# Side-by-side halves in the narrowest score and value products of a fused attention + FFN kernel

## The chip, the cores and the metric

The kernel runs on one core of one Trainium2 chip. The metric is the device time of one execution in microseconds (us), lower is better. The median of three runs of the kernel before is 1170.11 us.

Engine names as the profile has them: PE is TensorE (matrix products; PEld is its weight load), DVE is VectorE, ACT is ScalarE, POOL is GpSimd, SP is SyncE, whose queue here issues the DMA transfers.

## The reference

Block-causal attention over 8 batches and 8 heads (576 tokens, head width 64, blocks of 64 tokens), followed by a feed-forward net (FFN) with a leaky ReLU:

```python
q, k, v: (8, 8, 576, 64) float32
scores = (1 / sqrt(64)) * q @ k^T                 # per batch and head
scores = where(pos_i // 64 >= pos_j // 64, scores, -1e9)
attn   = exp(scores - max(scores)); attn /= sum(attn) + 1e-9
x      = (attn @ v), heads side by side           # (4608, 512)
h      = x @ w_in                                 # (4608, 2048)
out    = maximum(0.01 * h, h) @ w_out             # (4608, 512)
```

## The kernel before

**Precision by halves.** Most products run in the fp32r type, in two or three terms: an operand is split into a rounded high part and a low part that holds the rest. `subtracting` (L250 on DVE, L251 on POOL) makes low parts, `copying` (L240/L243 on ACT, L241/L244 on DVE) high parts. Scores take two terms (`qs` against `kh` and against `kl`, L459), values two (`pth` and `ptl` against `vs`, whose 128 weight columns hold the high and the low part of v, L613), the FFN three per product (L712, L731). Some early products run in plain fp32 instead (L453, L603), which needs no split.

**Work items.** `work` lists 72 attention items: for the 8 heads of batch 0 first the lower 320 query tokens ("lo", items 0 to 7), then the upper 256 ("hi", 8 to 15), and then one item for each of the other 56 heads ("full", 16 to 71). A score row holds five query tiles t = 0 to 4, of 64, 128, 128, 128 and 128 tokens, which look at 64, 192, 320, 448 and 576 keys. Tiles 0 to 3 are scored in a first group, tile 4 in a second (the score PSUM tile `p_s` has two banks). After a group come mask (L470), row maximum (L477, DVE), exponent with row sums (L486, ACT), reciprocal (L501/L502, L505) and normalisation (L517 POOL, L518 DVE, L519 ACT). Then PE transposes the probabilities into `p_t` (L551), they are copied out (`pth`, `ptl`, or `ptf` in plain fp32), and the value products follow (L613, L603). The output of key block 0 with 128 query columns (tile 4 and tile 0, the `outer` products) goes to a `p_t` bank of its own, `x0`; the other four spans go to bank `x1`. The attention result is written to `xr` (`put_x`, L592 and L641), which the FFN reads.

**FFN.** 18 chunks of 256 tokens; each chunk has 8 units of 24 products of 256 columns (L712) and 12 of 512 columns (L731). A chunk may begin when the heads of its tokens are done.

**Weights.** They come as 64-bit numbers, in 32 pieces (16 of each matrix) of 512 KB, by way of three `raw` buffers (L361). Each piece is turned into float32 by four operations (L365, L368 on ACT, L369, L373 on DVE), then split into high and low parts. This goes on beside the "lo" and "hi" items.

**Order.** `Plan` takes all operations with ranks, durations and the engines that may do them, simulates the engines, and emits the instructions in the order that results, so that every engine's order is fixed before the kernel runs. While PE has nothing to do early on, it is kept running with dummy products (`fill`, L784). Constants such as `RL`, `RP` or `SL1` are offsets of ranks, in units of one attention item: a load of item i has rank i - RL. A second set of buffers (`second_stage`: `xr[1]`, `ptl`, `v_stage`, a second row of probability buffers) takes the place of the weight-staging buffers after the last piece. `HS` is the number of "hi" heads whose scores run in plain fp32. In "lo" items and those "hi" items q and k are stored twice over the 128 rows, and q is scaled in place by half the usual factor first (L243/L244 on `qk_in`).

Of the kernel before, what the change touches and what calls it, by code (L numbers as in the profile page):

```python
# [26 lines left out]
HS = 8  # L27
SIGNS = 4
# [5 lines left out]
RL = 3.85  # L34
RP = 0.396
RB = 0.255
RT = 1.189
RV = 1.756
RX = -1.367
RN = -0.808  # L40

LEAD = 2.089
LAG = 1.994
RS = 2.992
RG = -0.004
OFF1 = 5.088
SL1 = 12.185
AHEAD = -0.653

LAT = 1550  # L50
HOLD = 167.582
# [6 lines left out]
SLOW = 8000  # L58
JOINT = 0
# [164 lines left out]
def attention_ffn(ctx: ExitStack, tc: tile.TileContext, qk: bass.AP, v: bass.AP, w_in: bass.AP, w_out: bass.AP, out: bass.AP):  # L224
    nc = tc.nc
    B, H = qk.shape[0], qk.shape[1]
    DM, DFF = w_in.shape
# [41 lines left out]
    pth = fixed([P, 1600], F32R, "pth")  # L269
# [17 lines left out]
    kh = fixed([P, S], F32R, "kh", 2)  # L287
    kl = fixed([P, S], F32R, "kl", 2)
# [29 lines left out]
    def second_stage():  # L318
        stage.close()
        pool = ctx.enter_context(tc.tile_pool(name="late", bufs=1, reuse_waits="tile"))  # L320
        xr[1] = fixed([P, ND, S], F32, "xr1", None, pool)
        later["ptl"] = fixed([P, 1600], F32R, "ptl", None, pool)
        later["v_stage"] = fixed([P, NT, D], F32, "v_stage", None, pool)
        rows(1, pool)

    def weight_piece(num, rank, f, out_side, c0):
# [31 lines left out]
        if src.dtype != F32:  # L358

            def load():  # L360
                nc.sync.dma_start(shaped(raws[k], 2 * P), src.bitcast(I32))  # L361
# [3 lines left out]
                ("ACT", act(w, True) + 70, lambda: nc.scalar.activation(val(), top(), AF.Copy, scale=2.0**-112)),  # L365
                ("DVE+", dve(w), lambda: nc.vector.tensor_scalar_mul(val(), top(), 2.0**-112)),
# [19 lines left out]
    def attention(i):  # L386
# [25 lines left out]

        def load():
            if qa == 0:
                nc.sync.dma_start(qkt[:rows, :, :qe], qk[b, h, :rows, :, :qe])
# [4 lines left out]
        add([("SP", {"full": 475, "lo": 650, "hi": 1300}[kind], load)], r0 - RL, [], [qkey], lag=dma((qe - qa + ke) * rows * 4))  # L420
# [26 lines left out]
        def scores(tiles):  # L447
            banks = [bank for bank, _ in tiles]
            for y, (b, (t, ap, k0, k1, c)) in enumerate(tiles):
                first, last = b not in banks[:y], b not in banks[y + 1 :]  # L450
                cols = slice(q0[t], q0[t] + P)
                if plain_s:
                    go = lambda ap=ap, cols=cols, k0=k0, k1=k1, first=first, last=last: nc.tensor.matmul(  # L453
                        ap, qkt[:rows, 0, cols], qkt[:rows, 1, k0:k1], start=first, stop=last
# [3 lines left out]
                kk = (kh[z], kl[z])[c]  # L458
                go = lambda ap=ap, cols=cols, kk=kk, k0=k0, k1=k1, first=first, last=last: nc.tensor.matmul(  # L459
                    ap, qs[z][:, cols], kk[:, k0:k1], start=first, stop=last  # L460
# [3 lines left out]
        def softmax(tiles, mms, masks, r):  # L464
# [16 lines left out]

            def exponent(t, ap, flat):
# [3 lines left out]
                nc.scalar.activation(  # L486
                    o, ap[: qn[t]], AF.Exp, bias=nm[z][: qn[t], t : t + 1], scale=1.0, accum_out=sums[z][: qn[t], t : t + 1]
# [10 lines left out]
        def normalise():  # L498
            ts = sorted(t for t, _, _ in done)
            a, e = ts[0], ts[-1] + 1  # L500
            one = lambda: nc.scalar.activation(rec[z][:, a:e], sums[z][:, a:e], AF.Copy, bias=EPS)  # L501
            two = lambda: nc.vector.tensor_scalar_add(rec[z][:, a:e], sums[z][:, a:e], EPS)  # L502
            sk, rk = [("sum", z, t) for t in ts], [("rec", z, t) for t in ts]
            add([("DVE+", 75, two), ("ACT", 110, one)], r0, sk, rk)
            add([("DVE", 120, lambda: nc.vector.reciprocal(rec[z][:, a:e], rec[z][:, a:e]))], r0, [], rk)  # L505
# [16 lines left out]
        lay = order_a[kind]  # L522
# [4 lines left out]
        else:  # L527
            mms = [(at[t][0], (t, at[t][1], 0, kw[t], c)) for t, c in turns[kind]]
# [286 lines left out]
```

## Time and profile before

| | |
|---|---|
| median of 3 runs | 1170.11 us (1169.79 to 1174.19) |
| the profiled execution | 1170.27 us, of which 1168.5 us is the span of the trace |
| PE busy | 1159.0 us (99%), 7734 products and as many weight loads |
| ACT, DVE, POOL busy | 649.0, 622.7 and 432.8 us |
| chain that ended last | 96% PE |
| PE clock granted | 0.999 of full speed |
| first FFN product | 50.1 us |
| last transfer of weights and batch 0 | until about 122 us |
| last value products of attention | about 1014 us |

How to read the rows: a group of instructions is given as line, engine, operation, destination <- sources, shape (partitions x elements), count, then busy microseconds and the mean ns of one. In rows of a timeline the first number is the start in us from the beginning of the span, the second how long the merged instructions took. Products are pipelined, so the distance from start to start says what one costs, not its own duration. Rows of windows give the busy time and instruction count of PE, PEld, DVE, ACT and POOL in that stretch, then the granted PE clock, the busy share of the DMA engines and GB/s.

### The profile page before, as it was taken

Reading aid. Unit: us, or ns where it says so; the run is one execution under the profiler, and the core shown is the slowest. Engines: PE = TensorE matmul, PEld = TensorE weight load, DVE = VectorE, ACT = ScalarE, POOL = GpSimd, SP = SyncE. Lnnn points to the kernel's source line nnn. Section 1 sums busy time; section 2 is a strip of 40 time slices with the busy share of each in tenths; the row PEclk is TensorE's granted clock in tenths of the full one; section 3 lists DMA queues with packets and bytes.
Section 4 is the critical chain, followed back from the end, with each engine's and each line's share of the span. In section 5 each row is a group of like instructions: output and inputs, shape, how many; then the busy total and the mean of one; then the engine's idle time right before and its main releaser. Section 6 shows DMA issues by size and latency. Waiting matters only on the chain.

```text
span 1168.5 us, 20725 instructions
## 1 busy us (share of the span) xinstructions
PE 1159.0 (99%) x7734; PEld 1053.7 (90%) x7734; DVE 622.7 (53%) x1606; ACT 649.0 (56%) x1641; POOL 432.8 (37%) x411
## 2 busy tenths in 40 slices
PE   8999999999999999999999999999999999999998
PEld 7878889899999999999999999999999999999997
DVE  6889988975555555535344555555555555200000
ACT  7888867765555555545455556565555555322222
POOL 2332444443443443434334344343343433222221
PEclk9999999999999999999999999999999999999999
DMA  7666322211212121111111111112111100000000
GB/s 225 218 220 229 124 67 79 87 62 53 71 47 70 33 70 53 66 32 60 38 45 47 50 53 65 41 51 64 52 65 52 54 29 25 2 19 3 16 19 19
DMA packets 38950, 78.16 MB, mean 67 GB/s; under 512 B 3520, under 2 KB 24000, under 8 KB 38848
## 3 DMA queue, kind: packets, MB, share of 16 engines
q1 hardware_dynamic: 38848, 76.82, 20.4%
q8 instruction: 61, 1.00, 0.3%
q14 instruction: 41, 0.34, 0.1%
HBM read 67.37 MB, written 9.44 MB: 66 GB/s over the span
## 4 chain that ended last, share of the span: by engine, by line
PE 96%; DVE 1%; DMA 1%; ACT 1%; issue 0%; SPq 0%; POOL 0%; ACTq 0%
PE p_h L712 34%; PE p_o L731 34%; PE p_t L551 9%; PE p_s L459 8%; PE p_t L613 7%; PE p_t L603 2%; PE p_s L453 2%; PE p_o L784 1%; PE p_h L453 0%; DMA qk_in<-in_qk 0%; DMA v_stage<-in_v 0%; DVE nm L477 0%; ACT prow L486 0%; DVE ptl L250 0%; DVE qs L436 0%
## 5 line engine op out<-in xcount | busy, mean ns | idle before, releaser
L712 PE MATMUL p_h<-xh,wih 128*128 128x256 f32 x1152 | 327.8, 285 | 0.0
L712 PE MATMUL p_h<-xl,wih 128*128 128x256 f32 x1152 | 321.1, 279 | 0.5 <-DVE xl L250 0.5
L712 PE MATMUL p_h<-xh,wil 128*128 128x256 f32 x1152 | 320.6, 278 | 0.0
L251 POOL TENSOR_TENSOR gl<-g,gh 128x512 fp32r<-128x512 f32 x138 | 181.1, 1312 | 298.5 <-ACT gh L240 199.2
L486 ACT ACTIVATE prow<-p_s,nm 128x192 f32<-128x192 f32 (+4 forms) x308 | 160.5, 527 | 139.7 <-DVE nm L477 137.2
L712 PEld LDWEIGHTS p_h<-xl,wih 128*128 128x128 f32 x1152 | 217.3, 189 | 8.6 <-DVE xl L250 0.8
L712 PEld LDWEIGHTS p_h<-xh,wih 128*128 128x128 f32 x1152 | 216.7, 188 | 8.1 <-issue 0.4
L712 PEld LDWEIGHTS p_h<-xh,wil 128*128 128x128 f32 x1152 | 216.9, 188 | 0.0
L719 ACT ACTIVATE g<-p_h 128x512 f32<-128x512 f32 x144 | 85.6, 595 | 213.4 <-PE p_h L712 202.1
L517 POOL TENSOR_SCALAR prow<-prow,rec 128x576 f32<-128x576 f32 (+3 forms) x121 | 88.0, 730 | 310.3 <-DVE rec L505 282.6
L731 PE MATMUL p_o<-woh,gh 128*128 128x512 f32 x576 | 183.3, 399 | 0.0
L731 PE MATMUL p_o<-woh,gl 128*128 128x512 f32 x576 | 179.4, 393 | 0.0
L731 PE MATMUL p_o<-wol,gh 128*128 128x512 f32 x576 | 179.3, 393 | 0.0
L477 DVE TENSOR_REDUCE nm<-p_s 128x1 f32<-128x192 f32 (+4 forms) x308 | 140.1, 486 | 4.7
L551 PE MATMUL p_t<-ident,prow 128*128 128x128 f32 x960 | 130.2, 273 | 1.2 <-DVE xr L592 0.5
L731 PEld LDWEIGHTS p_o<-woh,gl 128*128 128x128 f32 x576 | 108.2, 188 | 24.3
L731 PEld LDWEIGHTS p_o<-wol,gh 128*128 128x128 f32 x576 | 108.2, 188 | 23.9
L250 DVE TENSOR_TENSOR ptl<-p_t,pth 128x512 fp32r<-128x512 f32 (+1 forms) x224 | 118.8, 567 | 16.8 <-ACT pth L240 14.3
L551 PEld LDWEIGHTS p_t<-ident,prow 128*128 128x128 f32 x960 | 110.0, 141 | 12.6 <-issue 1.9
L592 DVE TENSOR_TENSOR xr<-p_t,xr 64x64 f32<-64x64 f32 x112 | 50.2, 449 | 126.8 <-ACT xr L240 121.6
L240 ACT CAST pth<-p_t 128x384 fp32r<-128x384 f32 (+3 forms) x190 | 86.1, 499 | 39.8 <-PE p_t L551 39.6
L251 POOL TENSOR_TENSOR kl<-qk_in,kh 128x576 fp32r<-128x576 f32 x55 | 85.3, 1551 | 22.5 <-ACT kh L240 17.9
(78 smaller groups left out, 1561.7 us busy)
## 6 DMA issues: line engine op xcount, KB each, us to landing
qk_in<-in_qk SPq DMA_DIRECT2D x56, 576.0 KB, 3.7
v_stage<-in_v SPq DMA_DIRECT2D x56, 160.0 KB, 2.2
out<-ob SPq DMA_DIRECT2D x35, 256.0 KB, 2.3
raw<-in_w_in SPq DMA_DIRECT2D x16, 512.0 KB, 4.6
raw<-in_w_out SPq DMA_DIRECT2D x16, 512.0 KB, 3.9
qk_in<-in_qk SPq DMA_DIRECT2D x8, 320.0 KB, 4.0
qk_in<-in_qk SPq DMA_DIRECT2D x8, 288.0 KB, 3.7
vf<-in_v SPq DMA_DIRECT2D x8, 160.0 KB, 3.2
```

The lines of the kernel that those rows point to most:

```text
L240: one = lambda: nc.scalar.copy(dst(), src())
L250: ("DVE+" if sb else "DVE", dve(n), lambda: nc.vector.tensor_sub(dst(), one(), two())),
L251: ("POOL", pool2(n), lambda: nc.gpsimd.tensor_sub(dst(), one(), two())),
L459: go = lambda ap=ap, cols=cols, kk=kk, k0=k0, k1=k1, first=first, last=last: nc.tensor.matmul(ap, qs[z][:, cols], kk[:, k0:k1], start=firs ...
L477: [("DVE", dve(kw[t]), lambda t=t, ap=ap, flat=flat: nc.vector.tensor_reduce(nm[z][: qn[t], t : t + 1], ap[: qn[t]], axis=AX.X if flat els ...
L486: nc.scalar.activation(o, ap[: qn[t]], AF.Exp, bias=nm[z][: qn[t], t : t + 1], scale=1.0, accum_out=sums[z][: qn[t], t : t + 1])
L517: ("POOL", pool1(kw[t]), lambda: nc.gpsimd.tensor_scalar(p(), p(), by, 1.0, op0=ALU.mult, op1=ALU.mult)),
L551: return 27, lambda: nc.tensor.transpose(p_t[x][:, c : c + n], row(t, n, j * P, P), ident[:n, :n])
L613: nc.tensor.matmul(to, vs[z][:, j, :], src, start=start, stop=stop)
L712: nc.tensor.matmul(hh[:, i, :], w[:, d, f * P : (f + 1) * P], x[:, d, :], start=k == 0, stop=k == len(terms) - 1)
L719: add([("ACT", act(512), lambda: nc.scalar.activation(g, hh, AF.Prelu, alpha=0.01))], rank, [("h", z)], ["g"])
L731: nc.tensor.matmul(p_o[m], a[:, i, m * P : (m + 1) * P], w[:, 2 * u + i, :], start=u == 0 and k == 0, stop=u == NU - 1 and k == 5,)
```

## The change

1. **Side by side.** From attention item 26 on (`SIDE = 26`, so for 46 of the 56 "full" items) the score product of tile 0 (64 keys) and the `outer` value product (128 columns) are each issued as one matmul instead of two: the moving operand takes the high and the low part next to each other (128 columns for the scores, 256 for the values), which go to separate columns of PSUM. A `tensor_reduce` on DVE adds the halves. For that, `kh`/`kl` become the tile `kk` and `pth`/`ptl` the tile `pt`, and tile 0 moves from the first score group to the second. `pt` as a whole now lies among the buffers of the second stage; `pth` was there from the start.
2. **Plain fp32 items.** The scaling of q in place is gone; the negated row maximum `nm` is scaled instead (one small operation per group, on DVE or ACT), and the exponent gets the scale as a parameter. `HS` goes from 8 to 6: two "hi" heads score by halves.
3. **Loads.** q and k of batch 0 are laid out so that each transfer is contiguous per partition, and "hi" items need one transfer instead of two; `w_in` is laid out so that a piece is one run of 4 KB per partition instead of four of 1 KB. The value load's rank moves from r0 - RL + 0.1 to r0 - RL + 5.916.
4. **Weight conversion.** The first step (L365) may also run on POOL.
5. **Ranks.** The offsets of the order are other numbers, so the whole order is planned anew.

```diff
-HS = 8
+HS = 6
-RL = 3.85  RP = 0.396  RB = 0.255  RT = 1.189  RV = 1.756  RX = -1.367  RN = -0.808
+RL = 4.905 RP = 0.424  RB = 0.336  RT = 1.081  RV = 1.547  RX = -2.354  RN = -0.271
-LEAD = 2.089 LAG = 1.994 RS = 2.992 RG = -0.004 OFF1 = 5.088 SL1 = 12.185 AHEAD = -0.653 HOLD = 167.582
+LEAD = 2.402 LAG = 1.993 RS = 2.38  RG = -0.063 OFF1 = 5.089 SL1 = 11.71  AHEAD = -2.327 HOLD = 130.395
+SIDE = 26
+VD = 5.916
...
-    pth = fixed([P, 1600], F32R, "pth")
-    kh = fixed([P, S], F32R, "kh", 2)
-    kl = fixed([P, S], F32R, "kl", 2)
+    kk = fixed([P, 2, S], F32R, "kk", 2)
...
-        later["ptl"] = fixed([P, 1600], F32R, "ptl", None, pool)
+        later["pt"] = fixed([P, 2, 1600], F32R, "pt", None, pool)
...
-            src = w_in[c0 : c0 + WIDE, fs].rearrange("(c p) f -> p c f", p=P)
+            src = w_in[f, :, c0 : c0 + WIDE]
...
                 ("ACT", act(w, True) + 70, lambda: nc.scalar.activation(val(), top(), AF.Copy, scale=2.0**-112)),
+                ("POOL", pool1(w), lambda: nc.gpsimd.tensor_scalar(val(), top(), 2.0**-112, 1.0, op0=ALU.mult, op1=ALU.mult)),
...
-            if qa == 0:
-                nc.sync.dma_start(qkt[:rows, :, :qe], qk[b, h, :rows, :, :qe])
+            if b:
+                nc.sync.dma_start(qkt, qk[b - 1, h])
             else:
-                nc.sync.dma_start(qkt[:rows, 0, qa:qe], qk[b, h, :rows, 0, qa:qe])
-                nc.sync.dma_start(qkt[:rows, 1, :ke], qk[b, h, :rows, 1, :ke])
+                o = {"lo": 0, "hi": 640}[kind]
+                nc.sync.dma_start(qf[:, : nq + ke], qk0[h, :, o : o + nq + ke])
...
-        add([("SP", 475, lambda: nc.sync.dma_start(vt(), v[b, h, :, :nv]))], r0 - RL + 0.1, ...)
+        add([("SP", 475, lambda: nc.sync.dma_start(vt(), v[b, h, :, :nv]))], r0 - RL + VD, ...)
...
         if plain_s:
-            add(copying(qe - qa, lambda: q_in, lambda: q_in, by=scale / 2), rp, [], [qkey])
...
+                if c == 2:      # both halves: 2 x 64 columns
+                    go = lambda ...: nc.tensor.matmul(
+                        ap, qs[z][:, cols], kk[z][:, :, k0:k1], start=first, stop=last)
...
+            if sides:
+                add([("DVE", dve(128), lambda: nc.vector.tensor_reduce(sides[0], sides[1], axis=AX.X, op=ALU.add))], r, [], [(sk, 0)])
...
+            if plain_s:
+                add([
+                    ("DVE+", 75, lambda some=some: nc.vector.tensor_scalar_mul(some, some, scale / 2)),
+                    ("ACT", 110, lambda some=some: nc.scalar.activation(some, some, AF.Copy, scale=scale / 2)),
+                ], r, [], [("nm", z, t) for t in ts])
...
+        side = kind == "full" and i >= SIDE
...
+            if side:
+                sides = [p_s[0:64, 0, 416:480], p_s[0:64, 0, 288:416].rearrange("p (c k) -> p k c", c=2)]
+                late.append((0, sides[0], (0,)))
+                turn.insert(1, (0, (0, p_s[:, 0, 288:416].rearrange("p (a b) -> p a b", a=2), 0, 64, 2)))
...
+            if side:
+                outer = [product(p_t[x0][:, : 2 * w], 0, slice(c, c + w), 0, True, True, True)]
+                one, two, three, four = values
+                add([("PE", [one[0], outer[0], one[1]])], rv, ptd + [vkey], [("t", x0), ("t", x1)])
+                values = [[two[0], four[0], two[1], four[1]], three]
+                add(
+                    [("DVE", dve(4 * BLK), lambda: nc.vector.tensor_reduce(
+                        p_t[x0][:, 4 * BLK : 6 * BLK], p_t[x0][:, : 4 * BLK].rearrange("p (c k) -> p k c", c=2), axis=AX.X, op=ALU.add
+                    ))], rx, [], [("t", x0)],
+                )
...
+        "side": ((3, 0, 0), (1, 1, 0), (2, 1, 192)),                        # order_a
+        "side": ((3, 0), (1, 0), (3, 1), (1, 1), (2, 0), (2, 1)),           # turns
```

More of the change, by code (lines that the diff above doesn't have):

```diff
@@ L25 @@
 CH = 256
-HS = 8
-SIGNS = 4
+HS = 6
+SIGNS = 3
 WIDE = 512
@@ L32 @@
 VALS = 3
[L34 to L48, printed above, removed]
+RL = 4.905
+RP = 0.424
+RB = 0.336
+RT = 1.081
+RV = 1.547
+RX = -2.354
+RN = -0.271
+LEAD = 2.402
+LAG = 1.993
+RS = 2.38
+RG = -0.063
+OFF1 = 5.089
+SL1 = 11.71
+AHEAD = -2.327
 LAT = 1550
-HOLD = 167.582
+HOLD = 130.395
 FILL = 235
@@ L223, in attention_ffn @@
 @with_exitstack
-def attention_ffn(ctx: ExitStack, tc: tile.TileContext, qk: bass.AP, v: bass.AP, w_in: bass.AP, w_out: bass.AP, out: bass.AP):
+def attention_ffn(ctx: ExitStack, tc: tile.TileContext, qk0: bass.AP, qk: bass.AP, v: bass.AP, w_in: bass.AP, w_out: bass.AP, out: bass.AP):
     nc = tc.nc
-    B, H = qk.shape[0], qk.shape[1]
-    DM, DFF = w_in.shape
+    B, H = v.shape[0], v.shape[1]
+    DFF, DM = w_out.shape
     ND = DM // P
@@ L453, in scores @@
                     go = lambda ap=ap, cols=cols, k0=k0, k1=k1, first=first, last=last: nc.tensor.matmul(
-                        ap, qkt[:rows, 0, cols], qkt[:rows, 1, k0:k1], start=first, stop=last
+                        ap, q_in[:, cols.start - qa : cols.stop - qa], k_in[:, k0:k1], start=first, stop=last
                     )
@@ L520, in normalising @@
             ]
-        lay = order_a[kind]
+        side = kind == "full" and i >= SIDE
+        order = "side" if side else kind
+        lay = order_a[order]
         tiles = [(t, scored(k)[:, c : c + kw[t]], (k,)) for t, k, c in lay]
@@ L527, in attention @@
         else:
-            mms = [(at[t][0], (t, at[t][1], 0, kw[t], c)) for t, c in turns[kind]]
+            mms = [(at[t][0], (t, at[t][1], 0, kw[t], c)) for t, c in turns[order]]
         if kind == "full":
@@ L606, in go @@
             def go():
-                src, to = (pth, later["ptl"])[half], dst
-                if split:
-                    src = src[:, 1088:1600].rearrange("p (a b) -> p a b", a=2)[:, :, 192:256]
+                src, to = later["pt"], dst
+                if split and not side:
+                    src = src[:, half, 1088:1600].rearrange("p (a b) -> p a b", a=2)[:, :, 192:256]
                     to = dst.rearrange("p (a b) -> p a b", a=2)
+                elif split:
+                    src = src[:, :, 1088:1600].rearrange("p c (a b) -> p c a b", a=2)[:, :, :, 192:256]
+                    to = dst.rearrange("p (c a b) -> p c a b", c=2, a=2)
                 else:
-                    src = src[:, cols]
+                    src = src[:, half, cols]
                 nc.tensor.matmul(to, vs[z][:, j, :], src, start=start, stop=stop)
+            if split and side:
+                return 2 * RATE * (cols.stop - cols.start), go
             return RATE * (cols.stop - cols.start), go
@@ L624, in attention @@
             c, w = ends[kind]
-            outer = [product(p_t[x0][:, :w], 0, slice(c, c + w), y, y == 0, y == halves[-1], kind == "full") for y in halves]
-            if kind == "full":
+            if side:
[7 more added lines that the diff above has]
+                    ))], rx, [], [("t", x0)],
+                )
+            elif kind == "full":
+                outer = [product(p_t[x0][:, :w], 0, slice(c, c + w), y, y == 0, y == 1, True) for y in halves]
                 one, two, three, four = values
@@ L631, in attention @@
             else:
+                outer = [product(p_t[x0][:, :w], 0, slice(c, c + w), y, y == 0, y == halves[-1]) for y in halves]
                 add([("PE", outer)], rv, ptd + [vkey], [("t", x0)])
@@ L634, in attention @@
         if kind == "full":
-            put_x(x0, 64, 0, 64)
+            put_x(x0, 5 * BLK if side else BLK, 0, 64)
         put_x(x1, 0, *tokens[kind])
@@ L638, in attention @@
             late = place(512, 576)
+            fold = 4 * BLK if side else 0
             for r in (0, 64):
                 add(
-                    [("DVE", dve(64), lambda r=r: nc.vector.tensor_add(late(), p_t[x0][r : r + 64, 0:64], late()))],
+                    [("DVE", dve(64), lambda r=r: nc.vector.tensor_add(late(), p_t[x0][r : r + 64, fold : fold + BLK], late()))],
                     rx, [("t", x0)], keys_of(512, 576),
@@ L776, in attention_ffn @@
             new = [("x", 1, h, y) for h in range(H) for y in (0, 1)] + [("p", 1, t) for t in range(NT)]
-            new += ["vt"] + [("ptl", g[0]) for g in tgroups["full"]]
+            new += ["vt"] + [(a, g[0]) for g in tgroups["full"] for a in ("pth", "ptl")]
             add([("POOL", 600, second_stage)], 0, [y for k in wkeys.values() for y in k] + [("x", 0, h, 1) for h in range(H)], new)
```

66 lines of the change are left out of this document (42 added, 24 removed).

## The prediction, made blind

> **What bounds the kernel now.** I read the page's totals, the PE clock and the shares of the chain first, then windows by stage, then PE's timeline inside a head, and last the groups of the other engines in the first 160 us.
>
> ```profile
> span 1168.5 us, 20725 instructions
> PE 1159.0 (99%) x7734; PEld 1053.7 (90%) x7734; DVE 622.7 (53%) x1606; ACT 649.0 (56%) x1641; POOL 432.8 (37%) x411
> ...
> PE   8999999999999999999999999999999999999998
> ...
> PEclk9999999999999999999999999999999999999999
> ...
> PE 96%; DVE 1%; DMA 1%; ACT 1%; issue 0%; SPq 0%; POOL 0%; ACTq 0%
> ```
>
> PE is busy to the end at the full clock, and the chain that ended last is PE for 96%. So a change is worth what it takes out of PE's sequence, plus what it takes out of the stretches where PE has nothing useful to do. The windows show where these lie.
>
> ```profile
> core 0: us, PE busy (x) PEld busy (x) DVE busy (x) ACT busy (x) POOL busy (x), PEclk, DMA share, GB/s
> 0.00:30.00 30.00, 26.76 (x151) 22.44 (x151) 18.37 (x58) 21.77 (x67) 6.70 (x23) 1.00 0.74 228
> 30.00:60.00 30.00, 30.00 (x206) 24.59 (x205) 26.01 (x66) 26.23 (x66) 9.24 (x7) 1.00 0.68 214
> 60.00:90.00 30.00, 30.00 (x176) 23.67 (x175) 24.76 (x54) 26.74 (x58) 12.25 (x10) 1.00 0.68 218
> 90.00:120.00 30.00, 30.00 (x185) 24.61 (x185) 27.79 (x62) 26.60 (x54) 9.78 (x7) 1.00 0.71 238
> ...
> 300.00:400.00 100.00, 100.00 (x682) 92.48 (x681) 55.86 (x153) 54.98 (x147) 41.84 (x39) 1.00 0.17 53
> ...
> 1000.00:1100.00 100.00, 100.00 (x661) 91.33 (x660) 9.81 (x20) 26.85 (x47) 21.89 (x17) 1.00 0.03 11
> ```
>
> The columns are busy us and counts of PE, PEld, DVE, ACT and POOL. From 300 us on PE is full and DVE is at 55.86 of 100: there PE's own instructions set the time and the other engines have room. In the first 120 us it is the other way round: ACT has 21.8 to 26.7 of 30 us and DVE 18.4 to 27.8, both with gaps only where one waits for the other, while PE, shown as full, is in part running dummy products (a row of 22 of them, from 9.91 us, stands below) and slow fp32 products. So the first stage goes at the pace of ACT and DVE; when it is done earlier, the FFN begins earlier and all that follows moves with it. Now what a short product costs:
>
> ```profile
> 600.05 0.45 PE L613 MATMUL p_t<-pth,vs 128*128 128x512 f32 x2
> ...
> 601.67 0.28 PE L712 MATMUL p_h<-xh,wih 128*128 128x256 f32 x1
> 601.78 0.28 PE L712 MATMUL p_h<-xl,wih 128*128 128x256 f32 x1
> ...
> 605.78 0.40 PE L459 MATMUL p_s<-kh,qs 128*128 128x448 f32 x2
> ...
> 606.89 0.31 PE L712 MATMUL p_h<-xh,wih 128*128 128x256 f32 x1
> ...
> 612.52 1.04 PE L551 MATMUL p_t<-ident,prow 128*128 128x128 f32 x8
> 613.31 0.38 PE L459 MATMUL p_s<-kh,qs 128*128 128x288 f32 x1
> ...
> 613.92 0.28 PE L712 MATMUL p_h<-xh,wih 128*128 128x256 f32 x1
> ```
>
> Products of 256 columns start 0.11 us apart (601.67, 601.78), which is 0.44 ns a column. The eight transposes of 128 columns take 613.31 - 612.52 = 0.79 us, about 0.10 each, where 128 columns alone would be 0.057: a narrow product is priced by its weight load, not by its columns. The first score group (605.78 to 606.89, 1.11 us) confirms it: two products each of 448, 64, 320 and 192 columns would be 0.90 us by columns; with at least 0.108 for every product it is 2 x 0.198 + 2 x 0.141 + 4 x 0.108 = 1.11, as measured. I use that rule: the larger of 0.44 ns x columns and 0.108 us.
>
> **The change, part by part.** *Side by side, on PE.* Scores: two products of 64 columns go (2 x 0.108), one of 128 comes in the second group (0.108, as 128 columns need only 0.057): -0.108 us. Values: the ten products from 600.05 to 601.67 hold two of 128 columns (2 x 0.108); one of 256 replaces them (0.113): -0.103. Per head -0.211 us, and 46 heads give **-9.7 us**. These stand in the middle of a full PE, so what is taken out is gained whole, as long as PE has other work ready behind it, which 100.00 of 100 us busy says. Bounds: 0 if only columns counted, against which the transposes speak; -0.324 a head or -14.9 us at most, if the merged products cost nothing beside their neighbours.
>
> [...]
>
> *Side by side, on DVE.* Two reductions per head come in. The nearest rows are the row maxima:
>
> ```profile
> L477 DVE TENSOR_REDUCE nm<-p_s 128x1 f32<-128x320 f32 x60 | 28.5, 474 | 0.1
> L477 DVE TENSOR_REDUCE nm<-p_s 64x1 f32<-64x64 f32 x60 | 12.8, 213 | 1.2
> ```
>
> Between 64 and 320 elements that is 1.02 ns an element, so 128 elements in come to 0.278 us and 256 to 0.409: 0.69 us a head, 31.6 us in all, which lifts DVE from 56 to about 60 of 100 us. It is hidden: values end at 601.67 and the next transposes, which need a `p_t` bank, come at 612.52, so the fold has ten microseconds. The longer second score group (a fold, the maximum of tile 0 and its exponent before the last normalisation) delays a head's transposes by some 1 us, while PE does FFN units. I take 0. If that cover went (PE standing for the fold), it would be up to 0.69 us a head. From below, no gain: nothing is taken from DVE.
>
> *Two "hi" heads by halves.* Scores of such a head in fp32:
>
> ```profile
> 107.57 0.75 PE p_s L453 x2
> 110.69 0.97 PE p_s L453 x4
> ```
>
> 0.75 + 0.97 = 1.72 us on PE. By halves it is 2 x 0.2 for 448 columns plus the second group, 613.31 to 613.92: 1.0. PE gains 2 x 0.7 = 1.4 us between 60 and 120 us, where it is full. But q and k must be split for those heads: 0.41 for 256 columns of q (L243 below), by the slope to 320 columns 0.69 for 576 of k, and some 0.5 for the low part of q, 1.6 us of ACT and DVE each, 3.2 together (the low part of k may run on POOL).
>
> *First stage, ACT and DVE.*
>
> ```profile
> L365 ACT ACTIVATE val<-raw 128x512 f32<-128x512 f32 x30 | 20.2, 673 | 2.6 <-DMA raw<-in_w_in 1.8 <-DMA raw<-in_w_out 0.7
> L243 ACT ACTIVATE qk_in<-qk_in 128x256 f32<-128x256 f32 x7 | 2.9, 412 | 0.0
> L243 ACT ACTIVATE qk_in<-qk_in 128x320 f32<-128x320 f32 x6 | 2.8, 467 | 4.7 <-DMA qk_in<-in_qk 4.7
> ...
> L502 DVE TENSOR_SCALAR rec<-sums 128x1 f32<-128x1 f32 x12 | 1.8, 150 | 0.8 <-ACT prow L486 0.7
> ...
> L517 POOL TENSOR_SCALAR prow<-prow,rec 128x448 f32<-128x448 f32 x4 | 3.1, 777 | 9.7 <-ACT g L719 8.1 <-DVE rec L505 1.5
> ```
>
> Scaling in place goes: 8 x 0.467 and 8 x 0.412 at ACT's price, 7.0 us (a few on DVE, cheaper). Scaling `nm` comes: one for each "lo" item, two for each of six "hi" items, 20 at the price of the nearest tiny DVE operation, 0.150: 3.0 us. In the "lo" part that is -3.7 + 1.2 = -2.5 us over two engines that share the flexible work, so -1.2 us of time. The wait for an operation on the way to the first exponent stays, since `nm` is scaled after the maximum.
>
> L365 may go to POOL: 0.673 us off ACT for each piece, about 0.85 on POOL (0.777 for 448 columns). Some 13 of the 32 pieces fall before 50 us if they are spread evenly over 120; if half go, 4 us leave ACT, 2 us of time when shared. But POOL and DVE get in each other's way:
>
> ```profile
> 118.73 1.43 POOL L251 TENSOR_TENSOR kl<-qk_in,kh 128x576 fp32r<-128x576 f32 x1
> ...
> 119.77 0.94 DVE L373 SCALAR_TENSOR_TENSOR val<-val,raw 128x512 int32<-128x512 int32 x1
> ...
> 125.10 0.67 DVE L373 SCALAR_TENSOR_TENSOR val<-val,raw 128x512 int32<-128x512 int32 x1
> ```
>
> The same L373 takes 0.67 us alone and 0.94 when it starts inside a POOL operation that ends at 120.16. So I count half: **-1.0**, with 0 and -2.5 as ends. [...]
>
> *Loads.* The beginning:
>
> ```profile
> 0.74 0.66 SPq L415 DMA_DIRECT2D qk_in<-in_qk  x1
> ...
> 2.08 0.55 SPq L415 DMA_DIRECT2D qk_in<-in_qk  x1
> ...
> 4.24 0.47 ACT L243 ACTIVATE qk_in<-qk_in 128x320 f32<-128x320 f32 x1 [2.23 <-DMA qk_in<-in_qk]
> ...
> 7.20 0.47 ACT L243 ACTIVATE qk_in<-qk_in 128x320 f32<-128x320 f32 x1 [2.48 <-DMA qk_in<-in_qk]
> ...
> 9.91 4.22 PE L784 MATMUL p_o<-ident 128*128 128x128 f32 x22
> ```
>
> The second q/k load is issued at 2.08 behind the first v load and ACT gets it at 7.20; head 0 starts its scores after 0.47 us of scaling. With v after both q/k loads, SP issues it 0.6 us earlier, 128 KB less stand ahead of it, and neither head waits for a scaling: 0.5 us for head 0, about 2 for head 1. Afterwards loads are hidden (ACT waited 4.7 us for `qk_in` in all, both at the start, and 2.6 before L365, for `raw`), so longer runs of `w_in` and half the issues for "hi" buy little. I take **-1.0** for the start, ends 0 and -2.5. v later: its user is the value product late in the item, and SP sends whatever buffer is free; nothing queued behind it is urgent. 0, up to +1 if it comes late in the "lo" part.
>
> *pt in the second stage.* The first "full" items can't copy `pth` until the staging buffers are gone; before, only `ptl` waited. PE has FFN units there. 0, ends -1 and +2. *New ranks.* They reorder everything; bounded by the idle that the first stage has: -3 to +3, taken as 0.
>
> Sum: side by side -9.7; two heads -1.4 on PE against +1.6 of time on ACT/DVE (3.2 shared by two), less 1.0 for the scalings of the "hi" part (-3.3 + 1.8, halved, about -0.8), so **-0.6** in all; "lo" scalings -1.2; POOL -1.0; start -1.0. Together -13.5 us on the profiled execution's own 1170.27 (span 1168.5 and 1.8 around it; the median of the runs is 1170.11): **1156.8 us**.
>
> **The rivals.** (a) *First stage unmoved or a little longer*: POOL blocks DVE, split "hi" heads and the later `pt` eat what the scalings gave. Only the merges count, less up to 4 us: 1160.6 to 1164.6. For it: DVE at 27.79 of 30 between 90 and 120 us. Against: ACT and DVE lose more work than they get.
> (b) *First stage much shorter*: half the pieces' L365 leaves ACT undisturbed, order better, -8 us there: 1152, down to 1148. For it: ACT at 26 of 30 for 90 us and POOL at 9 to 12. Against: DVE is as full.
> (c) *Width alone counts*: merging leaves PE's columns as they are, the 9.7 us do not come, 1166.5. Against: the 0.79 us for eight transposes. [...]
> (d) *PE waits for the fold* (the other side): the `x0` bank or `p_s` stays taken for the folds, and PE stands for them in each head. At 0.69 us x 46 = 31.6 this gives 1188; from (13.5 + 5.9) / 46 = 0.42 us a head it is slower by over 0.5%, from 0.29 no faster. Against: the ten microseconds between values and next transposes, and DVE at 56%.
>
> **How the numbers follow.** 0.5% of the time, 5.9 us, is about what a measurement can tell from no change: faster means under 1164.3, slower over 1176. Forecast (1153 to 1160): 0.53. (a) 0.22, of which 0.02 ends within 0.5%. (b) 0.15. (c) 0.04, within. (d) 0.06, half of it slower, half within. So faster 0.88, same 0.09, slower 0.03. The range leaves out (c), (d) and the last 0.06 of (a) and (b): 1149 to 1164.
>
> **What would show it.** PE: 92 products fewer, dummy products aside; first score group of a late head 0.89 us, second 0.72, values nine products in 1.51. DVE in 300 to 400 us near 60, PE still 100. First FFN product at 47 to 48 us instead of 50. Wrong would be: the same start-to-start times for merged as for separate products, gaps of PE before transposes or scores with DVE as releaser, or a first stage that ends later than before, with L369 and L373 longer than 0.7 us on average.

## The result and the profile after

The changed kernel takes 1157.55 us (median of four runs, 1155.87 to 1159.38) beside 1169.95 of the kernel before: ratio 0.9886, 95% interval 0.9873 to 0.9900. A second set of runs gave 1157.70 and 0.9879 (0.9863 to 0.9895). The forecast was 1156.8, in a range of 1149 to 1164. The profiled execution is the slowest of the four, 1159.38 us; this page is of it.

The page of the changed kernel:

```profile
span 1157.3 us, 20580 instructions
PE 1146.9 (99%) x7646; PEld 1043.7 (90%) x7646; DVE 711.2 (61%) x1765; ACT 647.0 (56%) x1605; POOL 392.8 (34%) x394
...
PE 93%; DMA 2%; DVE 2%; ACT 2%; issue 0%; SPq 0%; ACTq 0%; DVEq 0%
```

PE is still full. The span is 11.2 us shorter, PE has 88 products fewer (92 from the merges, 4 dummies more), and DVE is 88.5 us busier. The folds are 32.1 us of that (19.2 + 12.9, below), the slower low part of q is 27.6 (48.7 to 76.3, at the end), and work moved to DVE from POOL, which went from 432.8 to 392.8 us.

Windows of the changed kernel (columns as ahead of the prediction), and then four of the kernel before that were not shown:

```profile
0.00:30.00 30.00, 27.32 (x166) 22.39 (x167) 20.53 (x65) 21.35 (x70) 9.65 (x28) 1.00 0.71 237
...
60.00:90.00 30.00, 28.80 (x163) 22.14 (x162) 27.12 (x55) 25.47 (x56) 9.23 (x8) 1.00 0.63 203
...
120.00:150.00 30.00, 27.93 (x183) 24.91 (x182) 26.59 (x63) 23.98 (x64) 15.06 (x18) 0.94 0.29 94
150.00:180.00 30.00, 30.00 (x209) 28.02 (x208) 25.07 (x67) 20.01 (x54) 12.48 (x13) 1.00 0.26 82
180.00:210.00 30.00, 29.94 (x212) 27.85 (x211) 23.73 (x69) 22.40 (x62) 13.07 (x14) 1.00 0.20 60
210.00:240.00 30.00, 30.00 (x208) 27.84 (x208) 24.25 (x65) 24.29 (x64) 13.57 (x15) 1.00 0.26 86
240.00:270.00 30.00, 29.38 (x198) 26.65 (x197) 25.19 (x65) 19.22 (x54) 11.88 (x13) 1.00 0.24 76
...
300.00:400.00 100.00, 100.00 (x681) 92.56 (x679) 71.33 (x180) 57.69 (x149) 35.22 (x36) 1.00 0.18 58
```

```profile
120.00:150.00 30.00, 28.80 (x192) 25.55 (x192) 27.76 (x67) 24.45 (x64) 13.52 (x18) 1.00 0.32 104
150.00:180.00 30.00, 29.47 (x207) 27.08 (x206) 25.10 (x65) 20.56 (x56) 11.21 (x12) 1.00 0.25 76
...
210.00:240.00 30.00, 29.22 (x198) 26.41 (x197) 26.70 (x67) 22.15 (x61) 12.57 (x13) 1.00 0.24 74
240.00:270.00 30.00, 30.00 (x207) 27.84 (x207) 18.92 (x51) 18.55 (x49) 13.47 (x14) 1.00 0.20 67
```

PE's column in the first 120 us is no better than before: 28.80 of 30 from 60 us (that loss is this execution's; another one of the same kernel, experiment 5, has 30.00 there). From 120 it even loses 2.07 us of 30 (before: 1.20), with the clock granted at 0.94. From 150 to 240 it gains: 30.00, 29.94 and 30.00, where before it had 29.47, 30.00 and 29.22. From 240 to 270, with the first merged heads (the first merged score product starts at 236.2), it loses 0.62, where before it lost nothing. From 300 on it is full, with DVE at 71.33 of 100 instead of the 60 forecast. Over the whole span PE's idle time did not shrink: 1168.5 - 1159.0 = 9.5 us before, 1157.3 - 1146.9 = 10.4 now. The gain is in PE's busy time.

PE's timeline inside a late head (values, first and second score group, with the row that follows each):

```profile
667.53 1.67 PE L644 MATMUL p_t<-pt,vs 128*128 128x512 f32 x9
...
669.04 0.62 PE L778 MATMUL p_o<-woh,gh 128*128 128x512 f32 x2
...
674.56 1.08 PE L468 MATMUL p_s<-kk,qs 128*128 128x448 f32 x6
675.47 1.04 PE L578 MATMUL p_t<-ident,prow 128*128 128x128 f32 x8
...
679.81 0.38 PE L468 MATMUL p_s<-kk,qs 128*128 128x288 f32 x1
...
680.52 0.63 PE L778 MATMUL p_o<-woh,gh 128*128 128x512 f32 x2
```

The nine value products end after 669.04 - 667.53 = 1.51 us (before 1.62). The first score group takes 675.47 - 674.56 = 0.91 (before 1.11), the second, with its one merged product, 680.52 - 679.81 = 0.71 (before 0.61). That is -0.11, -0.20 and +0.10: -0.21 us a head.

### The profile page after: what moved, and what is told of

Same layout as the page of the kernel before. It is cut to its first block, busy times and chain, and to the rows that moved or that the text cites. A ratio compares the mean times of both kernels' runs of the same rounds, so it can differ in the third digit from the quotient of the medians.

```text
span 1157.3 us, 20580 instructions
## 1 busy us (share of the span) xinstructions
PE 1146.9 (99%) x7646; PEld 1043.7 (90%) x7646; DVE 711.2 (61%) x1765; ACT 647.0 (56%) x1605; POOL 392.8 (34%) x394
## 4 chain that ended last, share of the span: by engine, by line
PE 93%; DMA 2%; DVE 2%; ACT 2%; issue 0%; SPq 0%; ACTq 0%; DVEq 0%
PE p_o L778 33%; PE p_h L759 33%; PE p_t L578 9%; PE p_s L468 7%; PE p_t L644 7%; PE p_t L631 2%; DMA raw<-in_w_in 1%; PE p_o L831 1%; PE p_s L457 1%; DMA raw<-in_w_out 1%; ACT prow L505 1%; DMA qk_in<-in_qk 1%; DVE qs L440 0%; DVE nm L488 0%; DVE pt L252 0%
## 5 line engine op out<-in xcount | busy, mean ns | idle before, releaser
L253 POOL TENSOR_TENSOR gl<-g,gh 128x512 fp32r<-128x512 f32 x108 | 144.6, 1339 | 296.6 <-ACT gh L242 204.4
L505 ACT ACTIVATE prow<-p_s,nm 128x320 f32<-128x320 f32 (+4 forms) x308 | 160.0, 527 | 131.2 <-DVE nm L488 130.2
L536 POOL TENSOR_SCALAR prow<-prow,rec 128x448 f32<-128x448 f32 (+2 forms) x134 | 89.1, 670 | 326.6 <-DVE rec L524 234.7
L488 DVE TENSOR_REDUCE nm<-p_s 128x1 f32<-128x320 f32 (+4 forms) x308 | 138.0, 487 | 3.5
L252 DVE TENSOR_TENSOR pt<-p_t,pt 128x512 fp32r<-128x512 f32 (+1 forms) x224 | 120.0, 568 | 24.6 <-ACT pt L242 22.7
L578 PE MATMUL p_t<-ident,prow 128*128 128x128 f32 x960 | 132.7, 275 | 1.1 <-DVE prow L537 0.5
L468 PE MATMUL p_s<-kk,qs 128*128 128x288 f32 (+2 forms) x592 | 113.8, 319 | 2.5 <-ACT prow L505 2.5
L242 ACT CAST pt<-p_t 128x256 fp32r<-128x256 f32 (+3 forms) x184 | 82.2, 488 | 51.7 <-PE p_t L578 48.0
L468 PEld LDWEIGHTS p_s<-kk,qs 128*128 128x128 f32 x592 | 90.8, 190 | 6.7 <-ACT prow L505 3.6
```

The lines of the kernel that those rows point to most:

```text
L242: one = lambda: nc.scalar.copy(dst(), src())
L252: ("DVE+" if sb else "DVE", dve(n), lambda: nc.vector.tensor_sub(dst(), one(), two())),
L253: ("POOL", pool2(n), lambda: nc.gpsimd.tensor_sub(dst(), one(), two())),
L468: go = lambda ap=ap, cols=cols, c=c, k0=k0, k1=k1, first=first, last=last: nc.tensor.matmul(ap, qs[z][:, cols], kk[z][:, c, k0:k1], start= ...
L488: [("DVE", dve(kw[t]), lambda t=t, ap=ap, flat=flat: nc.vector.tensor_reduce(nm[z][: qn[t], t : t + 1], ap[: qn[t]], axis=AX.X if flat els ...
L505: nc.scalar.activation(o, ap[: qn[t]], AF.Exp, bias=nm[z][: qn[t], t : t + 1], scale=scale / 2 if plain_s else 1.0, accum_out=sums[z][: qn ...
```

## The experiments

**1. All but the merges.**

```diff
-SIDE = 26
+SIDE = 72
```

> The changed kernel with SIDE = 72, so no item has its halves side by side; all else (order of the first stage, loads, scalings, two heads by halves) stays. Theory (each narrow product costs PE the 0.108 us of its weight load, folds are hidden, the first stage gave little): 46 x 0.211 = 9.7 us come back, 1167.3 us. Rival 'width alone counts': about 0.1 us come back, 1157.6. Rival 'the folds cost PE what the merges save': the same 1157.6. If the first stage gave the 3.8 us of the prediction and the merges the rest: 1166.3.

Measured: 1166.36 us (ratio to the kernel before 0.9968, 0.9955 to 0.9980). All else is worth 3.4 us; width alone and costly folds, both at 1157.6, are out.

**2. The merges alone.** The kernel before with `kk`, `pt`, the side-by-side products and folds. One small thing comes along in every run with the new code, experiment 1 included: in the second score group both high halves are issued ahead of both low ones.

```diff
+SIDE = 26
...
+            if side:
+                outer = [product(p_t[x0][:, : 2 * w], 0, slice(c, c + w), 0, True, True, True)]
```

> The kernel before with the side-by-side products of items 26 to 71 alone: its own ranks, loads, scalings and plain fp32 heads (pt lies in the second stage, as the merges need it). Theory: 1170.1 - 9.7 = 1160.4 us. Rival 'width alone counts': 1170.2. Rival 'pt in the second stage holds up the first full items': 1161 to 1163, with PE idle between 125 and 160 us longer than in the kernel before.

Measured: 1160.34 us (0.9915, 0.9902 to 0.9929), 9.5 us less than before. 9.5 + 3.4 = 12.9, against 12.4 and 14.2 for the whole in the two sets of runs, each beside its own runs of the kernel before: within the noise, the two halves of the change add up. PE has 29.39 of 30 us from 120 to 150, more than the 28.80 before, so `pt` in the second stage held nothing up there.

**3. One more narrow product.**

```diff
                 turn.insert(1, (0, (0, p_s[:, 0, 288:416].rearrange(...), 0, 64, 2)))
+                turn.insert(3, (1, (0, p_s[:, 1, 288:352], 0, 64, 0)))
```

> The changed kernel, and in each of the 46 late items one more score product of 64 columns (high half of tile 0 again, into PSUM columns nobody reads) among the four of 288 columns in the second group. Theory (price = weight load): 46 x 0.108 = +5.0 us, 1162.5. [...] Rival 'width alone counts' (64 x 0.44 ns = 0.028 us): +1.3 us, 1158.8.

Measured: 1161.29 us (0.9926, 0.9914 to 0.9939), 3.6 to 3.7 above the changed kernel's two medians, and 4.7 to 5.5 by the ratios, each taken against its own runs of the kernel before. That is far from the +1.3 of 'width alone counts', and the theory's +5.0 lies between the two readings. The trace says more closely what one product costs. The second score group of a late head, and the row behind it:

```profile
679.74 0.38 PE L468 MATMUL p_s<-kk,qs 128*128 128x288 f32 x1
...
680.57 0.62 PE L779 MATMUL p_o<-woh,gh 128*128 128x512 f32 x2
```

With one more product of 64 columns the group takes 680.57 - 679.74 = 0.83 us instead of the 0.71 above: 0.12 us for it, and over 34 late heads the mean rises from 0.70 to 0.82. The period of heads, below, gives 0.11.

**4. No folds.** `sides` and the `tensor_reduce` of `x0` go, the products stay as wide; only the high half of them is read.

```diff
-                late.append((0, sides[0], (0,)))
+                late.append((0, p_s[0:64, 0, 288:352], (0,)))
...
-                    [("DVE", dve(4 * BLK), lambda: nc.vector.tensor_reduce(
-                        p_t[x0][:, 4 * BLK : 6 * BLK], ...
```

> The changed kernel without the two folds on DVE: the merged products stay as wide as they are, but of tile 0's scores and of the outer values only the high half is read (the low half is left out of the result). Theory (folds hidden): the same time, 1157.5, within 1 us, with DVE some 32 us less busy. Rival 'PE waits for the folds': up to 46 x 0.70 = 32 us less; from -2 us on it would be seen.

Measured: 1155.84 us (0.9875, 0.9860 to 0.9890), 1.7 us under the changed kernel's first median, more than the 1 us that theory allowed, but with a ratio inside the changed kernel's interval. The period of late heads says more.

These four, read by the period of late heads. Each pair of rows is the start of the value products of a head and of the head 18 later, in the trace of the kernel before, the changed one (with 667.53 above), and experiments 1, 2, 3 and 4:

```profile
679.34 0.45 PE L613 MATMUL p_t<-pth,vs 128*128 128x512 f32 x2
...
967.63 0.45 PE L613 MATMUL p_t<-pth,vs 128*128 128x512 f32 x2
```

```profile
951.64 0.74 PE L644 MATMUL p_t<-pt,vs 128*128 128x512 f32 x3
```

```profile
669.89 1.76 PE L644 MATMUL p_t<-pt,vs 128*128 128x512 f32 x10
...
957.49 1.76 PE L644 MATMUL p_t<-pt,vs 128*128 128x512 f32 x10
```

```profile
674.28 1.67 PE L634 MATMUL p_t<-pt,vs 128*128 128x512 f32 x9
...
958.32 1.67 PE L634 MATMUL p_t<-pt,vs 128*128 128x512 f32 x9
```

```profile
667.46 0.74 PE L645 MATMUL p_t<-pt,vs 128*128 128x512 f32 x3
...
953.61 1.67 PE L645 MATMUL p_t<-pt,vs 128*128 128x512 f32 x9
```

```profile
664.34 1.67 PE L643 MATMUL p_t<-pt,vs 128*128 128x512 f32 x9
...
948.38 1.67 PE L643 MATMUL p_t<-pt,vs 128*128 128x512 f32 x9
```

The period is (967.63 - 679.34) / 18 = 16.02 us before and (951.64 - 667.53) / 18 = 15.78 after; 15.98 without the merges, 15.78 with the merges alone, 15.90 with one more narrow product, 15.78 without the folds. So a 64-column product costs 0.11 us of PE's time, four times its columns (64 x 0.44 ns = 0.028 us); in late heads the folds cost nothing; and the change takes 0.23 us from each late head. The merges alone take 0.19 (against experiment 1) to 0.24 (experiment 2 against the kernel before), so such periods agree to about 0.04 us where the order around them differs.

The folds and their cover: first their rows in the changed kernel, then the windows from 700 to 980 us of the changed kernel and of experiment 4.

```profile
L664 DVE TENSOR_REDUCE p_t<-p_t 128x128 f32<-128x256 f32 x46 | 19.2, 418 | 9.2 <-PE p_t L644 9.2
...
L484 DVE TENSOR_REDUCE p_s<-p_s 64x64 f32<-64x128 f32 x46 | 12.9, 281 | 0.1
```

```profile
700.00:980.00 280.00, 280.00 (x1901) 259.07 (x1901) 198.59 (x498) 160.04 (x406) 94.83 (x95) 1.00 0.16 52
```

```profile
700.00:980.00 280.00, 280.00 (x1902) 259.11 (x1901) 172.12 (x434) 159.99 (x415) 99.25 (x103) 1.00 0.16 50
```

0.418 + 0.281 = 0.70 us a head, as forecast (0.409 + 0.278). DVE is 26.5 of 280 us less busy in experiment 4, and PE is at 280.00 in both. The folds themselves are about 12 of the 26.5 (17.7 heads of 0.70); without them the order around them is another too. Nearer the start it may be different: from 240 to 270 us PE has 30.00 in experiment 4, and 29.38 and 29.35 in the two traces of the changed kernel. So at the first merged heads the folds may cost PE some 0.6 us once.

**5 to 8. Parts of the first stage, each taken back under the changed kernel's ranks.** The base, run again:

> The changed kernel unaltered, as the base for the three others of this group: 1157.5 us by its own median, 1156.9 by adding what the merges alone (-9.5) and all the rest alone (-3.4) gave.

Measured: 1157.70 us (0.9879).

```diff
-                ("POOL", pool1(w), lambda: nc.gpsimd.tensor_scalar(val(), top(), 2.0**-112, 1.0, ...)),
```

> The changed kernel without POOL as a choice for the first step of weight conversion (13 of 32 pieces ran there). Theory (the prediction's term): +1.0 us. Rival 'POOL blocks DVE for what ACT saves': 0. Rival 'the order without it is better': -1 or less.

Measured: 1166.37 us (0.9953, 0.9939 to 0.9968): +8.7, far from all three expectations.

```diff
-HS = 6
+HS = 8
```

> The changed kernel with all eight hi heads in plain fp32 (HS = 8). The prediction's term: +0.6 us (PE 1.4 us more, ACT and DVE 3.2 us less between them). Rival 'PE bounds that stretch': +1.4 to +1.6. Rival 'ACT and DVE bound it': -1.6.

Measured: 1159.92 us (0.9901, 0.9887 to 0.9915): +2.2. The sign fits; the size is nearer to 'PE bounds that stretch' than to the prediction's 0.6, but the intervals overlap, and 2 us are about what they leave open.

```diff
         if plain_s:
+            add(copying(qe - qa, lambda: q_in, lambda: q_in, by=scale / 2), rp, [], [qkey])
             qkd = [qkey]
...
-                    ("DVE+", 75, lambda some=some: nc.vector.tensor_scalar_mul(some, some, scale / 2)),
-                    ("ACT", 110, lambda some=some: nc.scalar.activation(some, some, AF.Copy, scale=scale / 2)),
```

> The changed kernel with q scaled in place in the plain fp32 items (14 operations of 0.41 to 0.47 us on ACT, or 0.3 on DVE), and the 20 small scalings of nm left out. The prediction's terms: +1.2 in the lo part and +0.8 in the hi part, 2.0 us together. Rival 'ACT and DVE are not what paces the first stage, since they wait for raw transfers of up to 7 us there': 0.

Measured: 1166.21 us (0.9954, 0.9941 to 0.9968): +8.5, far from both.

**9. One instruction off DVE's queue.**

```diff
-                ("DVE+", ..., lambda: nc.vector.tensor_scalar_mul(p(), p(), by)),
+                ("DVE+", ..., lambda: (nc.scalar.mul if i == 16 and t == 2 else nc.vector.tensor_scalar_mul)(p(), p(), by)),
```

> The changed kernel with one instruction moved from DVE to ACT, at the same place of the order: the normalisation of tile 2 of item 16 (L537, 128 x 320), which took 1.42 to 1.61 us on DVE while a POOL subtraction of weights ran, and behind which stood the row maximum and the exponent that PE waited 2.0 us for. Everything else stays in its order. Theory (POOL holds DVE up, and that sets PE's longest wait): the wait falls from 2.0 to below 1 us, -1 to -1.5 us in all, and -3 where the wait was followed by a halved PE clock (0.66 granted between 130 and 135 us in the changed kernel's profile). Rival 'the wait is of PE's own order, the exponent is late anyhow': no change.

Measured: 1155.48 us (0.9866, 0.9851 to 0.9881), the fastest of all, 2.2 below the base; the intervals overlap, so the time alone doesn't show it. The trace shows the wait. Its chain in the changed kernel (POOL, DVE, ACT, PE, then the window behind it), and L537, PE's row and the window in experiment 9:

```profile
126.22 1.29 POOL L253 TENSOR_TENSOR wol<-val,woh 128x512 fp32r<-128x512 f32 x1
```

```profile
126.57 1.61 DVE L537 TENSOR_SCALAR prow<-prow,rec 128x320 f32<-128x320 f32 x1
128.10 0.74 DVE L488 TENSOR_REDUCE nm<-p_s 128x1 f32<-128x576 f32 x1
```

```profile
128.87 0.74 ACT L505 ACTIVATE prow<-p_s,nm 128x576 f32<-128x576 f32 x1 [1.14 <-DVE nm L488]
```

```profile
129.76 2.23 PE L468 MATMUL p_s<-kk,qs 128*128 128x448 f32 x8 [2.03 <-ACT prow L505]
```

```profile
130.00:135.00 5.00, 5.00 (x30) 4.93 (x30) 4.76 (x12) 3.50 (x9) 3.56 (x3) 0.66 0.00 2
```

```profile
124.61 0.55 ACT L537 ACTIVATE prow<-prow,rec 128x320 f32<-128x320 f32 x1
```

```profile
127.08 1.39 PE L468 MATMUL p_s<-kk,qs 128*128 128x448 f32 x8 [1.03 <-ACT prow L505]
```

```profile
130.00:135.00 5.00, 5.00 (x40) 4.72 (x39) 4.49 (x14) 4.34 (x16) 3.70 (x5) 1.00 0.39 127
```

In the changed kernel POOL subtracts weights until 127.51. L537, a normalisation that takes 0.55 us on ACT (and 0.39 on DVE at 192.07 us), stands on DVE until 128.18. Behind it waits the row maximum, behind that the exponent at 128.87, and PE has its scores only at 129.76 after 2.03 us of waiting. After the wait its clock was granted at 0.66 in the mean of the next five microseconds. With L537 on ACT the wait is 1.03 us and the clock stays at 1.00. So L537's 1.61 us on DVE did lengthen this wait: without them it is 1.00 us shorter than here, and 0.81 shorter than in the other trace of the changed kernel (1.84 us, experiment 5). That POOL held L537 up is read from the overlap: L537 began inside the POOL subtraction and ended 0.67 us after it, and the one of 0.39 us at 192.07 began ahead of POOL's next instruction (192.21). That the slow clock is gone because the wait is shorter is not shown, for the clock also stayed at 1.00 behind a wait of nearly the same length and in the same place in experiment 1:

```profile
128.62 1.39 PE L468 MATMUL p_s<-kk,qs 128*128 128x448 f32 x8 [1.95 <-ACT prow L505]
```

```profile
130.00:135.00 5.00, 4.74 (x42) 4.44 (x40) 4.40 (x12) 3.86 (x12) 4.28 (x3) 1.00 0.13 24
```

**10. Merges from the first full item on.**

```diff
-SIDE = 26
+SIDE = 16
```

> The changed kernel with the halves side by side in all 56 full items (SIDE = 16). If PE's sequence alone sets the time: 10 x 0.211 = -2.1 us, 1155.5. Rival 'DVE sets the pace in items 16 to 25' (24 to 27 of 30 us busy there): the folds add 10 x 0.70 = 7.0 us to DVE, PE waits for it, and the time rises by up to 5 us.

Measured: 1174.81 us (1.0030, 1.0020 to 1.0040): slower than before, and by 17 us than from item 26 on, far beyond either expectation. Windows, the longest wait of PE, and what DVE did ahead of it:

```profile
120.00:150.00 30.00, 25.00 (x159) 22.50 (x158) 24.38 (x56) 20.10 (x53) 13.27 (x17) 0.89 0.30 94
...
210.00:240.00 30.00, 23.22 (x112) 19.38 (x111) 21.14 (x57) 18.71 (x51) 10.68 (x11) 0.72 0.21 68
```

```profile
131.29 2.07 PE L468 MATMUL p_s<-kk,qs 128*128 128x448 f32 x6 [4.91 <-ACT prow L505]
```

```profile
127.15 2.14 DVE L243 CAST xh<-xr 128x1024 fp32r<-128x1024 f32 x1
```

PE has 25.00 of 30 us from 120 and 23.22 from 210, with clocks of 0.89 and 0.72: it stands for the exponent (4.91 us once), and the stretches with the gaps are those with a slow clock. It looks like the prediction's rival (d) at an earlier place, but the rank offsets were still those of the kernel that merges from item 26 on. Ahead of the longest wait the score fold had ended at 126.33; the row maximum stood behind a cast that took 2.14 us beside a POOL subtraction (0.69 in experiment 9), as in the chain above. So the folds' own time does not explain that wait. Folds on a DVE that has no room and offsets that don't fit would both leave PE waiting, and no run here parts them.

**11. The old layout of the loads.**

```diff
-            src = w_in[f, :, c0 : c0 + WIDE]
+            src = w_in[c0 : c0 + WIDE, fs].rearrange("(c p) f -> p c f", p=P)
...
+                nc.sync.dma_start(qkt[:rows, 0, qa:qe], qk[b, h, :rows, 0, qa:qe])
+                nc.sync.dma_start(qkt[:rows, 1, :ke], qk[b, h, :rows, 1, :ke])
```

> The changed kernel with the loads of q, k and w_in laid out as before (1 KB and 1280-byte runs, two transfers for a hi item); the later v loads stay. The prediction's term for the layout: 0 to +0.5 us, since loads are hidden. Rival 'raw transfers pace the first stage' (waits of 23 us of POOL and 9 of ACT for raw in the changed kernel): +2 us or more.

Measured: 1168.82 us (0.9976, 0.9965 to 0.9987): +11.1, on the side of the rival. Part of it lies at the very start, where PE has 25.43 of the first 30 us instead of 27.32; the rest has to be read with what follows.

**12. The new parts under the old ranks.**

```diff
-RL = 4.905 ... SL1 = 11.71  AHEAD = -2.327  HOLD = 130.395
+RL = 3.85  ... SL1 = 12.185 AHEAD = -0.653  HOLD = 167.582
...
-VD = 5.916
+VD = 4.861
```

> The changed kernel with the rank offsets of the kernel before (RL to AHEAD, SL1 and HOLD; v loads at the same rank as in the changed kernel). Leaving out one part of the first stage under the new offsets cost 8.5 to 11 us, although all parts together gave 3.4. Theory (offsets and parts belong together: the order is planned around the exact amounts of work, and any misfit makes PE wait between 90 and 250 us): the parts under the old offsets lose as well, 1162 to 1168. Rival 'the parts themselves bring the gain, whatever the offsets': 1157 to 1159. Rival 'the old offsets are the better ones': below 1157.

Measured: 1166.38 us (0.9967, 0.9955 to 0.9979): +8.7 to +8.8, inside the theory's range. The window from 120 to 150 us in experiments 6 and 12:

```profile
120.00:150.00 30.00, 25.51 (x158) 22.00 (x157) 24.42 (x58) 21.53 (x55) 16.81 (x16) 0.94 0.30 92
```

```profile
120.00:150.00 30.00, 23.75 (x154) 20.38 (x153) 27.13 (x61) 23.25 (x62) 17.57 (x21) 1.00 0.30 102
```

The changed kernel has 27.93 there; experiments 6, 8, 11 and 12 have 25.51, 25.99, 26.07 and 23.75. So each of them makes PE wait longer between the "hi" items and the first full ones, but that is only 1.9 to 4.2 us of what they lose; the rest lies elsewhere, in waits at other places and in PE's busy time. Under the old offsets the new parts lose (1166.38, beside 1160.34 for the merges alone under the same offsets), and leaving one part out under the new offsets costs more than all of them give together (3.4). So the 8 to 11 us of experiments 6, 8, 11 and 12 can't be read as the worth of one part. They hold, in a share that stays open, the price of offsets that go with other work; experiment 10, and 7 too, have to be read with the same care. The old parts under the new offsets were not run.

## Why the prediction was right, and where its steps were not

- *Side by side, on PE* (-9.7): right in size, and in that products count here and not columns. The period of late heads fell by 0.23 us, the merges alone gave 9.5 us, and one more product of 64 columns cost 0.11 to 0.12 us. The larger of 0.44 ns x columns and 0.108 us gets the differences right to 0.02 us a group. Whole groups come out a little longer than its sum: 1.51 us for the nine value products (1.46 by the rule), 0.71 for the second score group (0.62).
- Rival (c) is out by the same measurement: a product of 64 columns cost 0.11 to 0.12 us, where its columns alone would come to 0.028. That this price is the weight load's, as the prediction says, is the author's reading: the runs show the price, but as every product here has its own load (7646 of each), none parts the two.
- *Side by side, on DVE* (0): right for late heads, by experiment 4. The folds' own price was right to 0.01 us. That DVE would stand at 60 of 100 us was wrong (71.33): of the 15.5 us that came in, the folds are about 4.4 (0.70 us in each of 6.3 heads). How early in the kernel that cover still holds is open (experiments 4 and 10).
- *First stage* (-3.8 in all): the sum came out (-3.4 in experiment 1), but its working did not, so that agreement is in part luck. The step was "when it is done earlier, the FFN begins earlier and all that follows moves with it", with busy time added up and shared between two engines. That ACT and DVE have gaps "only where one waits for the other" was too narrow a reading: in the kernel before, DVE waited 11.9 us in seven places for PE's plain fp32 scores (L453). "First FFN product at 47 to 48 us" was wrong: 51.85, later than the 50.12 before. The last weight piece was converted 2.0 us earlier (L375 at 124.66, L373 at 126.64 before), but the last plain fp32 value products started 3.7 us later (123.67, before 119.94).

The changed kernel's first FFN row, and the rows of the low part of q in the kernel before, the changed one, experiment 6 (no conversions on POOL) and experiment 1 (13 conversions on POOL, no merges):

```profile
51.85 0.49 PE L759 MATMUL p_h<-xh,wih 128*128 128x256 f32 x1
```

```profile
L436 DVE SCALAR_TENSOR_TENSOR qs<-qk_in,qs 64x576 fp32r<-64x576 f32 x56 | 48.7, 870 | 2.1 <-ACT qs L243 0.4
```

```profile
L440 DVE SCALAR_TENSOR_TENSOR qs<-qk_in,qs 64x576 fp32r<-64x576 f32 x56 | 76.3, 1362 | 1.7
```

```profile
L439 DVE SCALAR_TENSOR_TENSOR qs<-qk_in,qs 64x576 fp32r<-64x576 f32 x56 | 76.9, 1373 | 1.9 <-issue 0.2
```

```profile
L440 DVE SCALAR_TENSOR_TENSOR qs<-qk_in,qs 64x576 fp32r<-64x576 f32 x56 | 45.0, 803 | 1.5
```

- *POOL* (-1.0): 13 of 32 pieces went there, 8.7 us off ACT (20.2 to 11.5), where 4 were forecast. The low part of q (L440) takes 1362 ns on average instead of 870, but not for these conversions: without them (experiment 6) it takes 1373, with them and without the merges (experiment 1) 803. The growth is in late heads (between 700 and 980 us its mean went from 754 to 1583 ns), where nothing is converted, and comes where merges and new offsets meet (808 in experiment 2). DVE's own two conversion operations grew only from 44.9 to 46.0 us. So rival (a), "POOL blocks DVE", is not borne out for the conversions. Single DVE instructions did take longer when they began inside a POOL one: L537 1.61 us instead of 0.39, the prediction's L373 0.94 instead of 0.67. That DVE stands still until POOL is done is not shown: L373 would then have taken 1.06 us (the 0.39 that POOL still ran, plus 0.67).
- *Two "hi" heads* (-0.6): the PE side (-1.4) was right or a little small (experiment 7: 2.2, not clear of the noise). The cost on ACT and DVE that was set against it was not seen. Where the sum says "less 1.0", it goes by the -0.8 behind it.
- *Start* (-1.0): the scores of heads 0 and 1 start at 3.70 and 5.88 us instead of 4.76 and 7.72, 1.1 and 1.8 us earlier (forecast: 0.5 and about 2), but nothing shows that this moved the end.
- What the rest of the change gained, by the traces: experiment 1 has a span 4.4 us shorter than before, 4.0 of it in PE's busy time (1159.0 to 1155.0) and 0.4 in its idle time (9.5 to 9.1). Between 150 and 240 us PE's idle time went from 1.31 us to 0.04, but from 120 to 150 it rose from 1.20 to 2.34. Of the busy time, the two "hi" heads are 1.4 us by the prediction's price. Where the remaining part lies stays open.
- *pt in the second stage* (0): right (experiment 2). *Loads* ("buy little"): not shown either way, as experiment 11 changes the offsets' fit too.

## What to carry to other kernels

In this kernel, where every product loads its own weights, narrow products went by their number and not by their columns: one of 128 columns for two of 64, and one of 256 for two of 128, took 0.21 us off a head, and one more of 64 cost 0.11 to 0.12. An estimate from the two measured prices (0.108 us a product, 0.44 ns a column) puts the limit at about 245 columns for both halves together; only 128 and 256 were tried. So count the products of such a kernel first, and give the fold to an engine with room. Before adding that fold, look at the engine's share in the stretch where it would run: here 0.70 us a head was free where DVE stood at 198.59 of 280 us with the folds in. When an order is planned ahead, a part taken out under the others' settings may show the misfit and not the part: trust a split only when its halves add up to the whole, as in experiments 1 and 2. And before a longer mean is put down to one cause, look at where in the kernel it grew: the low part of q grew where no weight is converted.

## What was not expected of the hardware

A wait of PE of only 2.03 us was followed by a granted clock of 0.66 in the mean of the next five microseconds; in experiment 9, behind 1.03 us, it stayed at 1.00. But the length of one wait does not decide it. Behind waits of 1.84 us (experiment 5) and 2.02 us (experiment 4) in the same place the clock fell as well (0.73 and 0.87 between 130 and 135 us); behind 1.95 us (experiment 1), 1.85 us (experiment 3) and even 2.49 us (experiment 12, at 139.82) it stayed at 1.00. What decides between them is not shown. The windows with the long waits of experiment 10 have clocks of 0.89 and 0.72. In the changed kernel the gap cost more than its own length: over five microseconds at 0.66 an estimated 1.7 us more (5 x 0.34). The granted clock was 0.50 to 0.51 from 130 to 133 us, and the eight transposes there take 133.35 - 131.79 = 1.56 us, instead of 0.79 in the kernel before at 612.52:

```profile
131.79 1.85 PE L578 MATMUL p_t<-ident,prow 128*128 128x128 f32 x8
133.35 0.41 PE L759 MATMUL p_h<-xh,wih 128*128 128x256 f32 x1
```
